# Gated linear attention by half chunks on 64x64 array tiles, ahead of a dropless mixture of experts

## The chip, the cores and the metric

The kernel runs on one core of one Trainium2 chip. The metric is the device time of one execution in microseconds (us). The median of three runs of the kernel before is 489.33 us (488.29 to 489.96).

## The reference

Two blocks stand one behind the other, all in fp32. The first is a recurrence over 768 positions for 4 batches and 8 heads of 48 numbers; its output, seen as 3072 rows of 384, goes through a router with 8 experts, of which each row takes the best one.

```python
B, H, S, D = 4, 8, 768, 48
for t in range(S):
    state = alpha[:, :, t, :, None] * state + np.einsum('bhd,bhe->bhde', k[:, :, t], v[:, :, t])
    y[:, :, t] = np.einsum('bhd,bhde->bhe', q[:, :, t], state)
x = y.transpose(0, 2, 1, 3).reshape(3072, 384)
logits = x @ w_gate                       # 384 x 8
expert_idx = argmax(logits, axis=1)       # gate_w: softmax probability of that expert
out = gate_w[:, None] * (np.maximum(x @ w1[e], 0) @ w2[e])   # e = expert_idx of the row; w1 384x1024, w2 1024x384
```

## The kernel before

**Chunks.** The recurrence is worked in chunks of C = 128 positions: 6 chunks for each of 4 batches, NT = 24 steps in all. With `ln` the logarithm of alpha (`logs`, L199, on ScalarE), one matmul with a triangular matrix gives its running sum inside the chunk (`cums`, L210, PSUM tile `cum`), from which ScalarE makes `icp` and `cp`, the exponentials of minus and plus that sum (L213, L214). GpSimd multiplies k by `icp` and q by `cp` into `kqb` (`operands`, L233, L234), where each head has 64 columns, 48 of them used. TensorE transposes both in pairs of heads (`transposes`, L241, tile `tp`), copied out to `kT` by ScalarE (L246) and to `qT` by VectorE (L244). A tile of 128 partitions holds two heads, one at partition 0 and one at partition 64 (DP = 64); NP = 4 such pairs make up the 8 heads.

**The attention of one step.** `scores` (L254) multiplies kT by qT, 128 x 128 for each head, into `sA` and `sB`. VectorE masks the one with the triangle (L258, `dA`), ScalarE copies the other (L260) and GpSimd masks it (L261, `dB`). `attend` adds into one PSUM tile `y` the product of the carried state `U` with qT (L274, not in the first chunk of a batch) and of v with the masked scores (L280), makes k times v for the state into `kvp` (L291), copies `y` to `yT` on VectorE (L295) and builds the next `U`: an addition on VectorE (L301, or L304 in the first chunk) and a multiplication on GpSimd (L302) with the decay `Eb` of the whole chunk. That decay is the last row of `cp` laid along the partitions: it goes to DRAM and comes back by three small transfers on ScalarE's queue (`decay_out` L218, `decay_in` L226).

**Rows and routing.** `rows` (L313, tile `xr`) turns `yT` back to rows of 384 and multiplies it by the gate's weights in one go, with the matrix `back`. `lgn` (L315, VectorE) sums the logits, `keep_rows` copies the row to `xs` (L320 ScalarE, L321 GpSimd) and stores it in DRAM (`x_rows`, L322). Groups of up to four steps are then routed: `choose` (L328 to L343) takes the best expert, `rank_products` (L348, L349) counts the places of the rows by two fp16 matmuls, `slots_of` (L356 to L364) makes slot numbers, and `one_hots` (L371, L372) makes two fp16 one-hot matrices for each step. After the last step their products (`tokens_of_slots`, L379, and L443 for the counts) give for each slot the row that belongs in it; `indices` (L390, L391) makes `g_idx` of it.

**Order.** Each engine runs its instructions in the order of the program, written out by hand in one loop. Step s of the loop issues loads, `logs(s+5)`, `cums(s+4)`, `operands(s+3)`, `transposes(s+2)`, `rows(s-1)`, `scores(s+1)`, `keep_rows(s-1)`, the decay transfers, `choose`, `attend(s)` and up to two `one_hots`. The loads of alpha, k, q and v (L194, L191: 128 x 8 runs of 192 bytes each), the stores of `x_rows` and the experts' weights (L167, L172) go through the one queue of the sync engine (SP).

**Experts.** The second part gathers rows by an indirect DMA on GpSimd (L499), transposes them (L522), copies them to `xT` (L524) and multiplies them with w1 (L528) and w2 (L553) of the expert; each result goes out by an indirect DMA (L559). Its first matmul needs `g_idx`, the last `x_rows` and the weights of expert 0, which the loop fetches whole at step 15.

Of the kernel before, what the change touches and what calls it, by code (L numbers as in the profile page):

```python
# [18 lines left out]
def kernel(  # L19
# [10 lines left out]
):  # L30

# [42 lines left out]

    consts = ctx.enter_context(tc.tile_pool(name="consts", bufs=1))
    ident = consts.tile([C, C], F32)
    cmask = consts.tile([C, C], F32)
    back = consts.tile([C, NP, D2 + E], F32)
    kqb = [consts.tile([C, 2, H, DP], F32, name=f"kqb{i}") for i in range(4)]
    vb = [consts.tile([C, H, DP], F32, name=f"vb{i}") for i in range(6)]  # L80
    Ub = [consts.tile([C, NP, DP], F32, name=f"Ub{i}") for i in range(2)]
    Eb = [consts.tile([C, NP], F32, name=f"Eb{i}") for i in range(5)]

    def first_consts():
        make_upper_triangular(nc, cmask[:], 1.0, diag=True)
        make_identity(nc, ident[:])
        for t in kqb:
            nc.vector.memset(t[:, :, :, D:], 0.0)
        for t in vb:
            nc.vector.memset(t[:, :, D:], 0.0)  # L90
        for t in Ub + Eb:
            nc.vector.memset(t[:], 0.0)

        for a in range(2):
            r = slice(a * DP, a * DP + D)
            nc.vector.tensor_copy(
                back[r, :, a * D : (a + 1) * D], ident[r, None, a * DP : a * DP + D].to_broadcast([D, NP, D]),
            )
            nc.vector.tensor_scalar_mul(back[r, :, D2:], back[r, :, D2:], -1.0)
# [48 lines left out]
    e_d = nc.dram_tensor("decay_rows", (NT, Dm), F32, kind="Internal").ap()  # L148
# [20 lines left out]

    def fetch2(ex):  # L170
        w2 = wpool.tile([C, FB, Dm], F32, name="w2")
        nc.sync.dma_start(w2[:], moe_w2[bass.ds(ex, 1)].rearrange("e (a p) d -> p (e a) d", p=C))  # L172
        return w2


    with tc.tile_pool(name="ld", bufs=6) as ld, \
         tc.tile_pool(name="work", bufs=2) as work, \
         tc.tile_pool(name="ps", bufs=1, space=PSUM) as ps, \
         tc.manual_schedule():
        st = {s: {} for s in range(NT)}  # L180

# [4 lines left out]
        def load(s, names):  # L186
            for n in names:
                src = rows_of({"a": alpha, "k": k, "q": q, "v": v}[n], s)
                if n == "v":
                    st[s][n] = vb[s % len(vb)]  # L190
                    nc.sync.dma_start(st[s][n][:, :, :D], src)  # L191
                else:
                    t = ld.tile([C, H, D], F32, name=n + "_sb", bufs=4 if n == "a" else 6)
                    nc.sync.dma_start(t[:], src)  # L194
                    st[s][n] = t
# [8 lines left out]
        def heads(t):  # L204
            return t[:].rearrange("s (h d) -> s h d", h=H)

        def cums(s):
            d = st[s]
            cum = ps.tile([C, Dm], F32, name="cum")
            nc.tensor.matmul(cum[:], lhsT=cmask[:], rhs=d["ln"][:], start=True, stop=True)  # L210
            d["icp"] = work.tile([C, Dm], F32, name="icp")
            d["cp"] = work.tile([C, Dm], F32, name="cp", bufs=3)
            nc.scalar.activation(d["icp"][:], cum[:], AF.Exp, scale=-1.0)  # L213
            nc.scalar.activation(d["cp"][:], cum[:], AF.Exp)  # L214

        def decay_out(s):
            if s % NB + 1 < NB:
                nc.scalar.dma_start(e_d[s : s + 1, :], st[s]["cp"][C - 1 : C, :])  # L218

        def decay_in(s):  # L220

            d = st[s]
            if s % NB + 1 < NB:
                d["E"] = Eb[s % len(Eb)]
                for a in range(2):
                    nc.scalar.dma_start(  # L226
                        d["E"][a * DP : a * DP + D, :], e_d[s].rearrange("(p a d) -> a d p", a=2, d=D)[a],
                    )

        def operands(s):  # L230
            d = st[s]
            kq = kqb[s % 4]
            nc.gpsimd.tensor_tensor(kq[:, 0, :, :D], d["k"][:], heads(d["icp"]), op=ALU.mult)  # L233
            nc.gpsimd.tensor_tensor(kq[:, 1, :, :D], d["q"][:], heads(d["cp"]), op=ALU.mult)  # L234
# [12 lines left out]

        def scores(s):
            d = st[s]
            sA = ps.tile([C, NP, C], F32, name="sA")  # L250
            sB = ps.tile([C, NP, C], F32, name="sB")
            for p in range(NP):
                for t, r in ((sA, 0), (sB, DP)):
                    nc.tensor.matmul(  # L254
                        t[:, p, :], lhsT=d["kT"][r : r + D, p, :], rhs=d["qT"][r : r + D, p, :], start=True, stop=True,
                    )
            d["dA"] = work.tile([C, NP, C], F32, name="dA")
            nc.vector.tensor_tensor(d["dA"][:], sA[:], cmask[:, None, :].to_broadcast([C, NP, C]), op=ALU.mult)  # L258
            d["dB"] = work.tile([C, NP, C], F32, name="dB")
            nc.scalar.copy(d["dB"][:], sB[:])  # L260
            nc.gpsimd.affine_select(  # L261
                d["dB"][:], d["dB"][:], compare_op=ALU.is_ge, fill=0.0,
                base=0, pattern=[[0, NP], [1, C]], channel_multiplier=-1,
            )

        def attend(s):

            d = st[s]
            c = s % NB
            y = ps.tile([C, NP, C], F32, name="y")  # L270
            if c > 0:
                for p in range(NP):
                    for r in (0, DP):
                        nc.tensor.matmul(  # L274
                            y[r : r + DP, p, :], lhsT=st[s - 1]["U"][r : r + D, p, :], rhs=d["qT"][r : r + D, p, :],
                            start=(p == 0), stop=False, skip_group_check=True,
                        )
            for p in range(NP):
                for i, r in enumerate((0, DP)):
                    nc.tensor.matmul(  # L280
                        y[r : r + DP, p, :], lhsT=d["v"][:, 2 * p + i, :], rhs=d["d" + "AB"[i]][:, p, :],
                        start=(c == 0 and p == 0), stop=True, skip_group_check=True,
                    )
            d["yT"] = work.tile([C, NP, C], F32, name="yT")
            kvp = ps.tile([C, NP * D + 4 * E], F32, name="kvp")
            kv = kvp[:, : NP * D].rearrange("r (p d) -> r p d", p=NP)
            ranked = [rank_products(g, kvp[:, NP * D : NP * D + len(g) * E]) for g in groups_of if g[-1] == s - 2]
            if c + 1 < NB:
                for p in range(NP):
                    for i, r in enumerate((0, DP)):  # L290
                        nc.tensor.matmul(  # L291
                            kv[r : r + DP, p, :], lhsT=kqb[s % 4][:, 0, 2 * p + i, :], rhs=d["v"][:, 2 * p + i, :D],
                            start=(p == 0), stop=True, skip_group_check=True,
                        )
            nc.vector.tensor_copy(d["yT"][:], y[:])  # L295
            if c + 1 < NB:
                d["U"] = Ub[s % len(Ub)]
                E_b = d["E"][:].unsqueeze(2).to_broadcast([C, NP, D])
                if c > 0:
                    acc = work.tile([C, NP, D], F32, name="acc")  # L300
                    nc.vector.tensor_tensor(acc[:], kv[:], st[s - 1]["U"][:, :, :D], op=ALU.add)  # L301
                    nc.gpsimd.tensor_tensor(d["U"][:, :, :D], acc[:], E_b, op=ALU.mult)  # L302
                else:
                    nc.vector.tensor_tensor(d["U"][:, :, :D], kv[:], E_b, op=ALU.mult)  # L304
            for r in ranked:
                slots_of(*r)

        def rows(s):
# [3 lines left out]
            for p in range(NP):  # L312
                nc.tensor.matmul(xr[:, p, :], lhsT=d["yT"][:, p, :], rhs=back[:, p, :], start=True, stop=True)  # L313
# [3 lines left out]
        def keep_rows(s):  # L317
# [4 lines left out]
            nc.sync.dma_start(x_d[s * C : (s + 1) * C, :], xs[:])  # L322
            del st[s]["xr"]

# [27 lines left out]
        def slots_of(g, pos):  # L352
# [10 lines left out]
            rc = work.tile([C, 2, n], F32, name="rc")  # L363
# [28 lines left out]

        def do(f, i, *a):
            if 0 <= i < NT:
                f(i, *a)

        nc.scalar.preload_act_table_set("natural_log_exp_and_others")
        for i in range(2):
            load(i, "akq")
        nc.gpsimd.memset(back[:], 0.0)  # L400
        for a in range(2):
            nc.scalar.dma_start(
                back[a * DP : a * DP + D, :, D2:], moe_w_gate.rearrange("(p a d) e -> a d p e", a=2, d=D)[a],
            )
        for i in range(2, 4):
            load(i, "akq")
        first_consts()
        hots = []
        for s in range(-5, NT + 1):
            do(load, s + 8 if s + 8 >= 4 else -1, "akq")  # L410
            do(load, s + 5, "v")
            do(logs, s + 5)
            do(cums, s + 4)
            do(operands, s + 3)
            do(transposes, s + 2)
            if s == NT:
# [247 lines left out]
```

## Time and profile before

| what | before |
|---|---|
| median of 3 runs | 489.33 us |
| profiled execution | 489.74 us, of which its span (first to last instruction) is 488.0 |
| TensorE matmul (PE) busy | 457.6 us, 94% of the span, 2881 instructions |
| PEld (weight loads), DVE (VectorE), ACT (ScalarE), POOL (GpSimd) busy | 297.4, 142.3, 103.2, 137.8 us |
| first `y<-dA` of step 0, of step 23 | 21.75 us, 156.6 us from the start |
| first gather of rows issued | 166.67 us |
| first product with w1 | 172.74 us |

All positions are microseconds from the start of the span. PE and PEld are the two halves of TensorE: each fp32 matmul stands as two MATMUL and two LDWEIGHTS instructions, while a transpose is one of each. A group such as `128*64 128x48` is a product with 128 rows and 64 columns of weights through which 48 columns are streamed. [...] durations of neighbours overlap: what a group costs is read from the distance between starts. SPq is the queue of the sync engine: it lists how long the issue of each transfer took.

### The profile page before, as it was taken

How to read it: one execution, taken by the hardware profiler on the slowest of the kernel's cores; microseconds unless marked ns; L12 is line 12 of the kernel's file. 1: busy time of each engine (PE TensorE's matmuls, PEld its weight loads, DVE VectorE, ACT ScalarE, POOL GpSimd, SP SyncE). 2: the span in 40 equal slices, each digit the busy share in tenths (PEclk: the TensorE clock that was granted, in tenths of full speed). 3: DMA queues.
4: the chain of work that ended last, by engine and by line, in shares of the span. 5: the costliest groups of instructions: out<-in, count | busy, mean ns of one | idle time of the engine just before them, and what ended most of it. 6: DMA issues, size and time to landing. Idle time of an engine off the chain costs nothing.

```text
span 488.0 us, 7370 instructions
## 1 busy us (share of the span) xinstructions
PE 457.6 (94%) x2881; PEld 297.4 (61%) x2881; DVE 142.3 (29%) x391; ACT 103.2 (21%) x209; POOL 137.8 (28%) x226
## 2 busy tenths in 40 slices
PE   2999999999999389999999999999999999999992
PEld 0788888888898275555555555555555455555451
DVE  2344766665778421212401201101201201301100
ACT  3544544544421001101001111011111001101010
POOL 3556745555642270010124010016020020010020
PEclk9999999999999779999999999999999999999997
DMA  9999999889992151300726400537300040000000
GB/s 161 199 177 203 207 210 203 168 170 272 299 356 107 50 160 39 142 32 8 267 75 211 135 32 0 189 118 249 129 28 16 1 166 22 1 20 16 2 32 25
DMA packets 127213, 59.76 MB, mean 122 GB/s; under 512 B 110304, under 2 KB 121604, under 8 KB 127178
## 3 DMA queue, kind: packets, MB, share of 16 engines
q1 hardware_dynamic: 114818, 48.87, 39.6%
q0 software_dynamic: 3584, 10.34, 6.4%
q10 hardware_dynamic: 8776, 0.08, 1.0%
q8 instruction: 23, 0.38, 0.3%
q14 instruction: 12, 0.10, 0.1%
HBM read 49.70 MB, written 10.35 MB: 123 GB/s over the span
## 4 chain that ended last, share of the span: by engine, by line
issue 54%; PE 27%; POOL 11%; DVE 2%; DMA 2%; SPq 1%; ACT 0%; POOLq 0%; ACTq 0%
POOL out_dram L559 6%; POOL xg L499 5%; PE sA L254 5%; PE y L280 4%; PE tp L241 4%; PE xr L313 4%; PE cum L210 4%; PE y L274 4%; PE kvp L291 2%; SPq L194 1%; DMA a_sb<-in_alpha_dram 1%; DMA x_rows<-xs 1%; DVE yT L295 1%; DVE sc L330 0%; DVE dA L258 0%
## 5 line engine op out<-in xcount | busy, mean ns | idle before, releaser
L528 PE MATMUL hp<-xT,w 128*128 128x448 f32 (+2 forms) x402 | 148.4, 530 | 1.2 <-DVE xT L524 1.2
L553 PE MATMUL zp<-w,h_sb 128*128 128x384 f32 (+1 forms) x512 | 146.8, 488 | 0.0
L528 PEld LDWEIGHTS hp<-xT,w 128*128 128x128 f32 x402 | 77.4, 194 | 69.9 <-issue 65.0
L553 PEld LDWEIGHTS zp<-w,h_sb 128*128 128x128 f32 (+1 forms) x512 | 81.1, 177 | 62.4 <-issue 13.6
L559 POOL DMA_INDIRECT out_dram<-zo,g_idx x28 | 27.7, 988 | 251.7 <-ACT zo L558 251.7
L542 DVE TENSOR_SCALAR h_sb<-hp 128x448 f32<-128x448 f32 x32 | 20.0, 624 | 218.4 <-PE hp L528 218.4
L544 ACT ACTIVATE h_sb<-hp 128x448 f32<-128x448 f32 x32 | 17.4, 543 | 142.0 <-PE hp L528 142.0
L558 ACT ACTIVATE zo<-zp,gw 128x384 f32<-128x384 f32 x28 | 16.3, 581 | 133.6 <-PE zp L553 129.0
L210 PE MATMUL cum<-ln,cmask 128*128 128x384 f32 x48 | 24.7, 601 | 8.7 <-ACT cp L214 4.4
L499 POOL DMA_INDIRECT xg<-x_rows,g_idx x28 | 26.9, 960 | 12.2 <-issue 12.2
L241 PEld LDWEIGHTS tp<-ident,kqb 128*128 128x128 f32 x192 | 23.5, 146 | 7.9 <-issue 4.2
L254 PE MATMUL sA<-qT,kT 48*128 48x128 f32 x192 | 27.7, 285 | 0.0
L254 PE MATMUL sB<-qT,kT 48*128 48x128 f32 x192 | 27.7, 285 | 0.0
L233 POOL TENSOR_TENSOR kqb<-k_sb,icp 128x384 f32<-128x384 f32 x24 | 23.9, 996 | 8.8 <-ACT icp L213 8.6
L241 PE MATMUL tp<-ident,kqb 128*128 128x128 f32 x192 | 26.2, 282 | 0.0
L280 PE MATMUL y<-dA,vb 128*64 128x128 f32 x192 | 26.1, 279 | 0.0
L280 PE MATMUL y<-dB,vb 128*64 128x128 f32 x192 | 26.1, 279 | 0.0
L313 PE MATMUL xr<-back,yT 128*128 128x104 f32 x192 | 25.4, 275 | 0.7 <-DVE yT L295 0.5
L261 POOL TENSOR_SCALAR_AFFINE_SELECT dB<-dB 128x512 f32<-128x512 f32 x24 | 15.2, 634 | 37.3 <-ACT dB L260 23.8
L254 PEld LDWEIGHTS sA<-qT,kT 48*128 48x128 f32 x192 | 23.1, 187 | 2.6 <-issue 0.3
L313 PEld LDWEIGHTS xr<-back,yT 128*128 128x128 f32 x192 | 23.3, 192 | 1.5 <-issue 1.0
L234 POOL TENSOR_TENSOR kqb<-q_sb,cp 128x384 f32<-128x384 f32 x24 | 23.9, 996 | 0.0
(117 smaller groups left out, 403.0 us busy)
## 6 DMA issues: line engine op xcount, KB each, us to landing
w<-in_moe_w_dram SPq DMA_DIRECT2D x16, 1536.0 KB, 6.8
x_rows<-xs SPq DMA_DIRECT2D x24, 196.0 KB, 2.9
a_sb<-in_alpha_dram SPq DMA_DIRECT2D x24, 192.0 KB, 4.1
k_sb<-in_k_dram SPq DMA_DIRECT2D x24, 192.0 KB, 3.8
q_sb<-in_q_dram SPq DMA_DIRECT2D x24, 192.0 KB, 4.0
vb<-in_v_dram SPq DMA_DIRECT2D x24, 192.0 KB, 4.6
Eb<-decay_rows ACTq DMA_DIRECT2D x40, 0.8 KB, 3.0
xg<-x_rows,g_idx POOLq DMA_INDIRECT x28, 3.1
```

The costliest lines, as they stand in the source:

```text
L210: nc.tensor.matmul(cum[:], lhsT=cmask[:], rhs=d["ln"][:], start=True, stop=True)
L233: nc.gpsimd.tensor_tensor(kq[:, 0, :, :D], d["k"][:], heads(d["icp"]), op=ALU.mult)
L234: nc.gpsimd.tensor_tensor(kq[:, 1, :, :D], d["q"][:], heads(d["cp"]), op=ALU.mult)
L241: nc.tensor.transpose(tp[:, p, :], pair(kqb[s % 4][:, i], p), ident[:])
L254: nc.tensor.matmul(t[:, p, :], lhsT=d["kT"][r : r + D, p, :], rhs=d["qT"][r : r + D, p, :], start=True, stop=True,)
L280: nc.tensor.matmul(y[r : r + DP, p, :], lhsT=d["v"][:, 2 * p + i, :], rhs=d["d" + "AB"[i]][:, p, :], start=(c == 0 and p == 0), stop=True, ...
L313: nc.tensor.matmul(xr[:, p, :], lhsT=d["yT"][:, p, :], rhs=back[:, p, :], start=True, stop=True)
L499: nc.gpsimd.indirect_dma_start(out=xg[:, j, :], out_offset=None, in_=x_d[:, :], in_offset=bass.IndirectOffsetOnAxis(ap=i, axis=0),)
L528: nc.tensor.matmul(hp[:, c0:c1], lhsT=w1[:, a, f * C : (f + 1) * C], rhs=xT[:, a, c0:c1], start=(a == 0), stop=(a == DB - 1), skip_group_c ...
L542: nc.vector.tensor_relu(h[:, f, :cols], hp[:, :cols])
L553: nc.tensor.matmul(zp[i * m : (i + 1) * m, :], lhsT=h[:, f, c0 : c0 + m], rhs=w2[:, f, :], start=(f == 0), stop=(f == FB - 1), skip_group_ ...
L559: ins = nc.gpsimd.indirect_dma_start(out=out[:, :], out_offset=bass.IndirectOffsetOnAxis(ap=idx, axis=0), in_=zo[:], in_offset=None, bound ...
```

## The change

- **Half chunks.** A chunk of 128 positions is worked as two halves j of 64. Scores are 64 x 64 within a half; what the second half owes to the first goes through the state, which is now carried per half: `Ub` holds a state for each half, and k times v (`kv_ps`) is made for each half. The products `inter` (state times qT), `scores`, `kv` and v times scores are 16 matmuls each in place of 8, every one with at most 64 rows and 64 columns of weights and 64 (kv: 48) columns streamed. Their order runs over the four 64x64 tiles of the array in turn. `rows` makes 8 matmuls in place of 4 (64 columns of weights, 104 streamed).
- **Evacuation.** One VectorE instruction masks both heads' scores (`dAB`, 128 x 512); the ScalarE copy and the GpSimd mask are gone. `y` is copied by ScalarE (`results`). VectorE has one more addition in each step (`state`).
- **Decay.** The last row of `cp` is laid along the partitions by 8 matmuls with one streamed column each (`decays`) and one small ScalarE copy. The transfers through DRAM and the tensor `decay_rows` are gone.
- **Order.** kv of step s+1 and y of step s stand at the head of a step, `rows(s)`, the rank products and the routing at its end; `inter(s+1)`, which waits for the copy of `y(s)`, comes after transposes and `cums`. The store of a row is issued at the head of the next step, ahead of its loads; loads run four steps ahead with five buffers each.
- **Constant products.** `keep_busy(n)` issues n matmuls of a zero matrix (128 x 256) that nothing reads: 4 + 4 + 3 + 2 + 1 before the first steps and 11 after the last routing product, ahead of the experts.
- **First weights.** Expert 0's weights come in 12 + 8 parts, one in each step from 6 on (two from 18 on), not whole at step 15.
- **Tail.** The last step's order is written out anew.

The core of the diff:

```diff
+    HALVES = [(j, a) for j in range(2) for a in range(2)]
+    def at(j, a):
+        return DP * (a ^ j)
...
+        def decays(s):
+            last_ps = sums_tile()[:, Dm + 4 * E : Dm + 4 * E + NP]
+            for p in range(NP):
+                for a in range(2):
+                    h = (2 * p + a) * D
+                    nc.tensor.matmul(
+                        last_ps[half(a), p : p + 1], lhsT=cpb[s % 3][DP:, h : h + DP], rhs=ident[DP:, C - 1 :],
+                        start=True, stop=True, skip_group_check=True,
+                    )
+                nc.scalar.copy(st[s]["E"][:], last_ps)
...
+        def inter(s):
+            for p in range(NP):
+                for j, a in HALVES:
+                    if j or s % NB:
+                        nc.tensor.matmul(
+                            y_ps[at(j, a) : at(j, a) + DP, j, p, :],
+                            lhsT=Ub[s % 2][head(a), j, p, :], rhs=d["qT"][head(a), p, half(j)],
...
         def scores(s):
+                for j, a in HALVES:
                     nc.tensor.matmul(
-                        t[:, p, :], lhsT=d["kT"][r : r + D, p, :], rhs=d["qT"][r : r + D, p, :], start=True, stop=True,
+                        sc_ps[half(j), a, p, :], lhsT=d["kT"][head(a), p, half(j)], rhs=d["qT"][head(a), p, half(j)],
...
-            nc.scalar.copy(d["dB"][:], sB[:])
-            nc.gpsimd.affine_select(
...
+            nc.vector.tensor_tensor(
+                d["dAB"][:], sc_ps, m64[:, None, None, :].to_broadcast([C, 2, NP, DP]), op=ALU.mult,
+            )
...
+        def state(s):
+                nc.vector.tensor_tensor(U[:, 1, :, :D], kv_ps[:, 0, :, :], U[:, 0, :, :D], op=ALU.add)
...
+                nc.vector.tensor_tensor(acc[:], kv_ps[:, 1, :, :], U[:, 1, :, :D], op=ALU.add)
+        def results(s):
+            nc.scalar.copy(st[s]["yT"][:], y_ps)
...
+        for s in range(-5, NT - 1):
+            do(store_rows, s - 1)
+            loads(s)
+            if s + 1 >= 0:
+                attend(s)
+            do(state, s + 1)
+            if 0 <= s + 1 < NT and (s + 1) % NB + 1 < NB:
+                decay(s + 1)
+            do(decays, s + 2)
+            do(results, s)
+            do(transposes, s + 2)
+            if s >= 0:
+                do(cums, s + 4)
+                do(operands, s + 4)
...
+            do(inter, s + 1)
+            do(scores, s + 2)
...
+            for _ in range(min(len(hots), 2 if len(hots) > 2 else 1)):
+                one_hots(hots.pop(0))
...
+            do(rows, s)
+            do(keep_rows, s)
...
+            do(logs, s + 5)
...
+        keep_busy(11)
```

## The prediction

> **What bounds the kernel now.** I read the page's busy shares first, then its slices, then busy time by window, then TensorE's timeline of one step, the waits, and SP's timeline. The page:
>
> ```profile
> PE 457.6 (94%) x2881; PEld 297.4 (61%) x2881; DVE 142.3 (29%) x391; ACT 103.2 (21%) x209; POOL 137.8 (28%) x226
> ...
> PE   2999999999999389999999999999999999999992
> PEclk9999999999999779999999999999999999999997
> DMA  9999999889992151300726400537300040000000
> ```
>
> PE is full but for the start and a notch in slices 13 and 14 (159 to 183 us), where its clock falls too. In the first nine slices the DMA engines are full as well. By window (us; busy of PE, PEld, DVE, ACT, POOL; PE clock; DMA share; GB/s):
>
> ```profile
> 63.09:69.26 6.17, 6.17 (x84) 5.41 (x82) 3.19 (x7) 2.84 (x6) 3.19 (x5) 1.00 1.02 190
> ...
> 164.00:170.00 6.00, 0.33 (x2) 0.10 (x1) 1.23 (x7) 0.00 (x0) 2.72 (x3) 0.50 0.16 39
> 170.00:177.60 7.60, 6.64 (x18) 4.89 (x19) 1.11 (x2) 0.00 (x0) 5.77 (x7) 0.50 0.56 157
> ```
>
> The first window is one attention step: PE is never idle, no other engine passes 3.2 of 6.17. The experts begin at half the clock. In that step, on TensorE's timeline:
>
> ```profile
> 64.92 0.27 PE L280 MATMUL y<-dA,vb 128*64 128x128 f32 x1
> 64.93 0.27 PE L280 MATMUL y<-dB,vb 128*64 128x128 f32 x1
> 65.03 0.62 PE L291 MATMUL kvp<-vb,kqb 128*64 128x48 f32 x16
> 65.58 0.91 PE L210 MATMUL cum<-ln,cmask 128*128 128x384 f32 x2
> 66.33 1.04 PE L241 MATMUL tp<-ident,kqb 128*128 128x128 f32 x8
> 67.20 1.04 PE L313 MATMUL xr<-back,yT 128*128 128x104 f32 x8
> ```
>
> Two matmuls on different parts of the array start together (64.92, 64.93; the records say 6.7 ns apart) and the next two follow 0.109 later. Distances between first starts give the step: state products 1.02, y from scores 0.92, kv 0.55, cum 0.75, transposes 0.87, rows 0.97, scores 1.09; sum 6.17. At plain pace (8 pairs at 0.109; kv 8 pairs at 0.058; cum 2 x 0.32; transposes and rows 8 x 0.109) it is 5.48; the other 0.69 lies where the tile shape changes. So the attention is bound by TensorE's stream, and weight loads set its short products: kv streams 48 columns but its pairs run at the 0.058 of 64 weight columns.
>
> Second in line is the transfer queue. At 55 us SP issues one step's five transfers with no gap:
>
> ```profile
> 55.04 0.42 SPq L194 DMA_DIRECT2D a_sb<-in_alpha_dram  x1
> 55.50 0.70 SPq L194 DMA_DIRECT2D k_sb<-in_k_dram  x1
> 56.25 1.08 SPq L194 DMA_DIRECT2D q_sb<-in_q_dram  x1
> 57.43 0.81 SPq L191 DMA_DIRECT2D vb<-in_v_dram  x1
> 58.35 0.90 SPq L322 DMA_DIRECT2D x_rows<-xs  x1
> ```
>
> From 55.04 to 78.19 five such rounds take 23.15, so 4.63 a step: the floor of a step by transfers. At the start ACT waits for alpha, 10.6 us in five waits:
>
> ```profile
> ACT ln L199 <- DMA a_sb<-in_alpha_dram: 10.6, 5, 3.3
> ```
>
> [...]
>
> **The change, part by part.**
>
> *TensorE in a step.* inter, scores, kv and y become 32 instructions each, four tiles in turn. If four run together, 8 rounds at kv's 0.058: 0.46 each, 1.86 in all, against 3.09 at plain pace before (2 x 0.87, 0.90, 0.46). The unseen price has bounds: 0.053 a round (64 columns at the 0.109 per 128) and 0.116 (two tiles at a time). I take 0.058, since four matmuls and four loads at the seen 6.7 ns fit into it. decays adds 16 instructions in 8 pairs, 0.46. rows: 16 in 8 pairs of 104 columns, 0.089 by scaling 0.109: 0.71 against 0.87. cum and transposes stay. Sum 1.86 + 0.46 + 0.71 + 0.87 + 0.64 = 4.54; there are again four changes of shape, so 0.69 more: 5.23. Rank products move but keep their number.
>
> *Other engines in a step,* by mean durations. ACT: loses the dB copy (0.588) and three issues (0.24, 0.31, 0.46), gains the yT copy (0.59) and a small one (about 0.2, by the 128x8 copies): 3.4. DVE: loses the yT copy (0.689), gains one addition (0.349): 3.9 with routing. POOL: loses the select (0.634): 2.9. None passes 5.23, but order counts. ACT waits at xs for lgn, as it did before; behind xs stand ln, the small copy, yT and kT, on which inter and scores of the next step wait. In one step of four two one_hots (1.6) stand ahead of lgn; then inter and scores come some 0.5 late. With choose, 2 us on DVE ahead of the next state, I charge 0.2 a step (bounds 0 and 0.5): **5.43**.
>
> *Transfers.* 4.63 plus a part of 128 or 192 KB from step 6 on: 0.4 to 0.65 at the 200 to 300 GB/s of the page. That is 5.0 to 5.3: hidden behind 5.43, barely, until k and q end at step 16. Without that cover each 0.1 costs 1. The store, now at a step's head, waits on SP for xs and holds four loads behind it; they are wanted four steps later, some 21 us, so that costs nothing while the queue isn't behind. On POOL the decay product now goes ahead of the operands of step s+4, which have two steps until their transposes: nothing.
>
> *Start.* y of step 0 stood behind cum of step 4, the 14th load (its ln began at 17.48); now behind cum of step 3, the 11th (about 14.7), so 18.5 for 21.75: -3.2. The first row store stands on SP behind 31 loads (the 31st was issued at 31.1), lands about 35, and xs has two buffers: step 2 waits for it near 34, +1.5. The constant products cost 4 to 9 us of PE, covered by the 8.7 us that it idles before 12.2. Net -1.7.
>
> *Steps.* Before, y went from 21.75 (step 0) to 141.57 (step 20): 119.8, with three cheap batch heads. Now 20 x 5.43 = 108.6: -11.2. Steps 20 to 23 took 15.0. Two without cum are 5.43 - 0.75 = 4.7 each; the next has kv and y 0.92, a wait of 0.9 for y's copy, inter 0.5 and rows 0.9, so 3.2; 12.6 in all: -2.4.
>
> *Tail.* From the last y to the gather, 156.6 to 166.67, DVE's chain decides: yT, one_hots and slots stood ahead of lgn (161.1). Now ACT copies y and lgn comes ahead of slots: -1.0, bounds -2 and +0.5.
>
> *Clock.* 11 products are 22 instructions, 4.7 us at full clock, between the last routing product and the first turn, 6.1 us later. Warm, the first 18 hp products take 18 x 0.213 = 3.8 and not 6.2: -2.4. If they begin cold, they need up to 8.4 and delay the turns by as much as they save: bounds -2.7 and +0.5.
>
> *Experts:* untouched; the last weight part is issued long before its use.
>
> Sum: -1.7 - 11.2 - 2.4 - 1.0 - 2.4 = -18.7. From the profiled 489.74 (0.4 above the median, 1.7 outside the span) that is **471 us**.
>
> **Rivals.**
> - *No stalls:* DVE and ACT keep up and the store doesn't bite: steps of 5.2, 462. For it: idle engines; against it: waits in order. 0.15.
> - *Transfers or the ACT/DVE order become the bound:* steps of 5.8 up to step 20: +7.4, 478, or up to 484. For it: the full DMA share. With four tiles only partly together (0.07 a round) it comes to the same. 0.2.
> - *Four tiles do not run together* (slower): a round costs two pairs, 0.116, so 4 x 8 x 0.058 = 1.86 more in each of 23 steps, +43: 514[...]. It decides from 0.084 a round, 21 ns a start. Against it: pairs 6.7 ns apart. 0.13.
> - *Gain and cost even out* near that point: 0.04.
> - *Constant products do not warm the clock:* +2.4, inside the range.
>
> **How the numbers follow.** The forecast, 466 to 476, has 0.48. Range 458 to 489: below, no stall and steps at the transfer floor; above, the point of balance. Outside lie the slower case and some 0.05 below. A measurement here tells 0.3% (1.5 us) from no change. Faster 0.83, same 0.04, slower 0.13.
>
> **What would show it.** Rounds of four near 0.058, a step's y to the next at 5.4; y of step 0 near 19 and of step 23 near 141; xs waiting for lgn; SP still without gaps to step 15; full clock at the first hp. Rounds above 0.084, or PE waiting on loads in most steps, would prove me wrong.

## The result, and the profile after

The changed kernel is slower: 508.76 us, median of four runs (503.4 to 512.39), beside 488.84 for the kernel before on the same chip; the ratio is 1.0368 (95% interval 1.0282 to 1.0454). One of the four, 512.39, counts as a slow run, and the ratio leaves it out. The profiled execution took 507.91, its span is 506.1, which is 18.1 more than the 488.0 of before. The page, lines that answer to those shown of before:

```profile
PE 462.4 (91%) x5043; PEld 298.5 (59%) x5043; DVE 132.6 (26%) x398; ACT 106.2 (21%) x229; POOL 126.0 (25%) x205
...
PE   5997996988987788999999999999999999999993
PEclk8899998999997679999999999999999999999997
DMA  9998979899879215230255330255330040000000
```

TensorE is no longer full in the attention (many an 8 or 7 and one 6 in slices 2 to 16, where before had 9 from the second slice to the thirteenth), and its clock drops in more places. Its waits from 30 to 140 us (in all, times, longest):

```profile
PE cum L259 <- issue: 5.6, 2, 4.4
PE y L340 <- issue: 5.2, 4, 2.0
PE scp L330 <- issue: 2.7, 3, 1.4
...
PE cum L242 <- ACT Eb L265: 0.2, 1, 0.2
```

"issue" means that the engine waited for nothing that the profile shows. So TensorE waits, and, but for 0.2 us, not for another engine or a load that it names. The positions say where the 18.1 us are (us; y is the first product of v with the scores):

| stretch | before | after | difference | predicted |
|---|---|---|---|---|
| start to y of step 0 | 21.75 | 26.26 | +4.5 | -3.2, +1.5 later |
| y of step 0 to y of step 20 | 119.82 | 129.96 | +10.1 | -11.2 |
| y of step 20 to y of step 23 | 15.04 | 21.29 | +6.2 | -2.4 |
| y of step 23 to first product with w1 | 16.13 | 15.74 | -0.4 | -1.0 |
| first product with w1 to end of span | 315.3 | 312.9 | -2.4 | -2.4 |

Busy time by window (us from the start; busy of PE, PEld, DVE, ACT, POOL; PE clock; DMA share; GB/s), first of the twenty steps in the kernel before:

```profile
21.75:141.57 119.82, 119.74 (x1553) 104.00 (x1551) 74.53 (x180) 56.14 (x121) 68.96 (x138) 1.00 1.00 220
```

Then of the kernel after: the twenty steps, one undisturbed step, the step behind it, and steps 20 to 23.

```profile
26.26:156.22 129.96, 110.58 (x3327) 92.15 (x3322) 64.78 (x183) 58.54 (x139) 60.65 (x120) 0.98 0.86 196
69.63:74.91 5.28, 5.28 (x183) 4.46 (x178) 3.17 (x8) 2.80 (x7) 2.79 (x5) 1.00 0.92 173
74.91:86.28 11.37, 6.96 (x186) 5.64 (x180) 3.97 (x16) 3.04 (x8) 3.41 (x9) 0.85 0.92 253
156.22:177.51 21.29, 17.56 (x415) 15.70 (x409) 9.08 (x37) 3.92 (x9) 2.00 (x7) 0.66 0.49 162
```

An undisturbed step takes 5.28 with TensorE full, a little under the forecast 5.43. The next holds nearly the same products (186 MATMULs for 183) and takes 11.37. TensorE's timeline (start, duration, line, operation, and in brackets the idle time ahead with what ended it) of both:

```profile
69.63 0.66 PE L340 MATMUL y<-dAB,vb 64*64 64x64 f32 x32
70.12 0.58 PE L259 MATMUL cum<-ident,cpb 64*64 64x1 f32 x16
70.64 1.09 PE L278 MATMUL tp<-ident,kqb 128*128 128x128 f32 x8
...
74.91 0.66 PE L340 MATMUL y<-dAB,vb 64*64 64x64 f32 x32
75.41 0.57 PE L259 MATMUL cum<-ident,cpb 64*64 64x1 f32 x15
80.39 0.26 PE L259 MATMUL cum<-ident,cpb 64*64 64x1 f32 x1 [4.41 <-issue]
80.58 1.75 PE L278 MATMUL tp<-ident,kqb 128*128 128x128 f32 x7
```

The 32 MATMULs of y take 0.49 from first start to the next group (0.06 a round of four): four tiles do run together. But in the second step TensorE stands for 4.41 us in the middle of `decays`, ahead of the 16th of 16 alike instructions, whose operands had long been there, and again "issue" is all that the profile says. A line on the DMA queues that I had not read shows what it waited for. Before, then after (packets, MB, share):

```profile
q8 instruction: 23, 0.38, 0.3%
```

```profile
q8 instruction: 40, 0.66, 0.5%
```

23 packets of 0.38 MB are 16 KB each. TensorE's 2881 MATMUL and 2881 LDWEIGHTS are 5762 instructions, 256 for each of 22.5 packets; after, 10,086 in 40 packets. With the semaphore and control instructions of TensorE's queue the two traces have 5898 and 10,259 records, 23.04 and 40.07 times 256. So in these two traces TensorE's program came 256 instructions at a time. Numbering all these records in order, the stops of the kernel after stand at numbers 193 + 256 n, and between y of step 0 and y of step 23 no other gap from start to start is over 1.1 us; each stop ends 1.3 to 1.7 us after the end of an instruction packet:

```text
block starts  packet starts + takes  next block starts  stop there
 35.16         37.67 + 0.95            40.11              2.26
 68.75         70.24 + 1.38            72.90              0.12
 72.90         78.09 + 0.95            80.39              4.60
119.69        121.67 + 0.88           124.10              1.63
```

In each row the packet starts after the boundary before it is passed (1.49 to 5.19 us after): one block was fetched ahead. A step of the kernel before has some 164 instructions in 6.17 us, so a block lasts 8 to 11 us; a step after has 340 in 5.28, and its blocks, less their stops, last 2.7 to 4.9 at full clock. Between y of step 0 and of step 20, 15 stops at block ends of over 0.5 us make 22.4 us (from start to start); before has none.

### The profile page after: what moved, and what is told of

It reads as the page before. It is cut to its first block, busy times and chain, and to the rows that moved or that the text cites. A ratio compares the mean times of both kernels' runs of the same rounds, so it can differ in the third digit from the quotient of the medians.

```text
span 506.1 us, 11711 instructions
## 1 busy us (share of the span) xinstructions
PE 462.4 (91%) x5043; PEld 298.5 (59%) x5043; DVE 132.6 (26%) x398; ACT 106.2 (21%) x229; POOL 126.0 (25%) x205
## 4 chain that ended last, share of the span: by engine, by line
issue 55%; PE 30%; POOL 9%; DMA 2%; SPq 2%; DVE 1%; ACT 0%; POOLq 0%; ACTq 0%; DVEq 0%
POOL out_dram L675 5%; PE tp L278 5%; PE xr L373 4%; PE cum L242 3%; POOL xg L615 3%; PE scp L330 3%; PE scp L313 3%; PE y L303 3%; PE y L340 3%; PE xr L472 2%; PE cum L259 2%; SPq L227 1%; DMA k_sb<-in_k_dram 1%; PE hp L644 1%; DMA vb<-in_v_dram 1%
## 5 line engine op out<-in xcount | busy, mean ns | idle before, releaser
L675 POOL DMA_INDIRECT out_dram<-zo,g_idx x28 | 27.7, 990 | 250.1 <-ACT zo L674 232.6
L281 DVE COPY qT<-tp 128x512 f32<-128x512 f32 x24 | 16.6, 692 | 41.0 <-PE tp L278 41.0
L242 PE MATMUL cum<-ln,cmask 128*128 128x384 f32 x48 | 21.8, 539 | 4.3 <-ACT ln L231 4.1
L318 DVE TENSOR_TENSOR dAB<-scp,m 128x512 f32<-128x512 f32 x24 | 16.6, 692 | 29.2 <-PE scp L313 29.2
L373 PE MATMUL xr<-back,yT 128*64 128x104 f32 x384 | 23.9, 270 | 0.0
L340 PE MATMUL y<-dAB,vb 64*64 64x64 f32 x768 | 19.1, 233 | 5.2 <-issue 5.2
L259 PE MATMUL cum<-ident,cpb 64*64 64x1 f32 x384 | 15.5, 193 | 9.0 <-issue 9.0
L383 ACT COPY xs<-xr 128x384 f32<-128x384 f32 x24 | 11.5, 479 | 55.8 <-DVE lgn L378 30.9
L271 POOL TENSOR_TENSOR kqb<-q_sb,cpb 128x384 f32<-128x384 f32 x23 | 23.1, 1003 | 0.0
L303 PEld LDWEIGHTS y<-qT,Ub 48*64 48x64 f32 x704 | 14.3, 142 | 13.5 <-issue 9.2
L640 DVE COPY xT<-xtp 128x384 f32<-128x384 f32 (+1 forms) x32 | 14.8, 503 | 25.4 <-PE xtp L638 25.4
```

The source lines that it names most:

```text
L242: nc.tensor.matmul(cum, lhsT=cmask[:], rhs=d["ln"][:], start=True, stop=True, skip_group_check=True)
L259: nc.tensor.matmul(last_ps[half(a), p : p + 1], lhsT=cpb[s % 3][DP:, h : h + DP], rhs=ident[DP:, C - 1 :], start=True, stop=True, skip_gro ...
L271: (nc.gpsimd if s else nc.vector).tensor_tensor(kq[:, 1, :, :D], d["q"][:], heads(d["cp"]), op=ALU.mult)
L303: nc.tensor.matmul(y_ps[at(j, a) : at(j, a) + DP, j, p, :], lhsT=Ub[s % 2][head(a), j, p, :], rhs=d["qT"][head(a), p, half(j)], start=(p = ...
L340: nc.tensor.matmul(y_ps[at(j, a) : at(j, a) + DP, j, p, :], lhsT=d["v"][half(j), 2 * p + a, :], rhs=d["dAB"][half(j), a, p, :], start=(p = ...
L373: nc.tensor.matmul(xr[half(j), p, :], lhsT=d["yT"][:, j, p, :], rhs=back[:, j, p, :], start=True, stop=True, skip_group_check=True,)
```

## Experiments

"Supply" below is the theory that TensorE's instructions arrive too slowly. Its first rival is the prediction's own: four tiles that do not run together. That fell with the 0.06 a round above; what was to be tested is whether the supply makes the loss, and what slows it. The edits are given in short.

**1. The supply by itself.** A kernel of zero products alone: a stream of 64x64 products on four tiles, once without and once beside loads like the kernel's, and a stream of 128-column products on two tiles.

```diff
+ two(64); four(1024)                  # quiet
+ for i in range(84): load 128 x 8 runs of 192 bytes
+ four(1024); two(512)                 # beside the loads
```

> This kernel computes nothing of the reference: it runs streams of fp32 products of zeros on TensorE, 64 products of 128 columns on two tiles, 1024 products of 64 columns on the four 64x64 tiles with no transfer running, then 84 loads in runs of 192 bytes beside 1024 more of them, then 512 of 128 columns on two tiles. Theory A (TensorE's instructions come in blocks of 256, one block ahead, and a block takes longer to arrive than four tiles take to use it): the four-tile stream, 7 ns an instruction between the stops, stops once every 256 instructions also without transfers, for at least 0.5 us each, so a block takes 2.5 us or more in place of 1.9; beside the loads the stops grow to 2 to 4 us; the two-tile stream, 27 ns an instruction and 7 us a block, never stops. Theory B (the stops of the changed kernel are waits for other engines' data that the trace does not name): nothing waits here, so no stops, 1.9 us a block throughout.

TensorE's timeline in the quiet stretch, and windows of the quiet stream, the loaded stream and the two-tile stream (columns as above, without ACT):

```profile
22.84 2.09 PE L34 MATMUL t<-still 64*64 64x64 f32 x128 [1.64 <-issue]
26.84 2.09 PE L34 MATMUL t<-still 64*64 64x64 f32 x128 [1.91 <-issue]
30.57 2.09 PE L34 MATMUL t<-still 64*64 64x64 f32 x128 [1.64 <-issue]
```

```profile
20.00:40.00 20.00, 11.54 (x723) 10.85 (x715) 0.00 (x0) 0.00 (x0) 1.00 0.02 5
80.00:100.00 20.00, 11.04 (x591) 10.34 (x581) 0.00 (x0) 0.00 (x0) 0.91 0.87 171
140.00:160.00 20.00, 20.00 (x370) 20.00 (x368) 0.00 (x0) 0.00 (x0) 1.00 0.95 186
```

The stream goes in groups of exactly 128 MATMULs (with their loads 256 instructions), 14.6 ns from start to start on average (1.87 over 128), and then stops, with the DMA engines idle (share 0.02). A block takes 3.5 to 4.0 us here, 3.8 to 4.6 beside the loads. The two-tile stream, whose blocks need some 7.0 us, is full at a DMA share of 0.95. So a stop needs no other engine and no load: VectorE and GpSimd have x0 in these stretches, and the quiet one stops at a DMA share of 0.02.

**2. Long runs.** Alpha, k and q are read as if each step's 192 KB were one piece (leaves out that they belong to the right heads and rows, so that the experts also get other numbers of rows).

```diff
+ if t is not v: return the flat 128 x 384 block s
```

> The changed kernel, with alpha, k and q loaded as the same number of bytes from one stretch of DRAM, in runs of 1536 bytes and not 192 (so the positions and heads are mixed up: the output is that of other inputs); v as before. Theory A1 (a block of instructions comes late because its transfer queues behind the many small runs): the stops of TensorE at its blocks shrink from some 24 us in all to under 8, and y goes from step 0 to step 20 in some 112 us and not 130. Theory A2 (the block's own delay, from request to use, is enough): stops stay above 15 us. Theory B (waits for data): since loads land sooner, any stop that is a wait for a load goes.

535.48 us, most of the excess in added expert blocks; only the attention counts. Stops at block ends between y of step 0 and step 20 fell from 22.4 to 16.1 us (ten for fifteen), the time between the two stayed (131.0), with the clock halved in four stretches of it, where the kernel after has one and the start of a second (mean clock 0.92 from 26 to 150 us, for 0.98 from 26.26 to 156.22 in the kernel after). The DMA share was 0.61 for 0.86. Long runs alone don't mend it. I took this as a sign that the block's own delay does nearly all the harm, which run 5 corrected.

**3. The same stream in fewer instructions.** inter, scores, kv and y as 4 matmuls each with 256 (kv: 192) columns for 16 with 64 (leaves out the other pairs' weights: each product uses the first pair's). The columns streamed are the same; 8 instructions a product group instead of 32.

```diff
- for p in range(NP): for j, a in HALVES: matmul(y_ps[.., j, p, :], lhsT=v[.., 2p + a, :], rhs=dAB[.., a, p, :])
+ for j, a in HALVES: matmul(y_ps[.., j, :, :], lhsT=v[.., a, :], rhs=dAB[.., a, :, :])
```

> The changed kernel with the same tiles, the same reads, writes and waits and the same streamed columns, but each of the four groups of 16 products issued as 4 products of 256 (kv: 192) columns: it uses the first pair's weights for all four pairs, which leaves out the other pairs' products. TensorE's instructions fall from 340 to about 150 a step at the same array time. Theory A: no stop is left in the steps, y of step 0 to step 20 takes 104 to 112 us in place of 130, the clock stays full until the tail, and the time falls by 22 to 30 us, to 479 to 487. Theory B: the waits for data are all still there, so the time falls by under 6 us.

481.03 us, ratio 0.9832 (0.9795 to 0.987): 27.7 less than the kernel after and faster than the one before. Its windows, y of step 0 to step 20 and one step, and its waits from 123 to 140 us:

```profile
26.20:137.61 111.41, 103.90 (x1474) 72.16 (x1466) 65.37 (x182) 57.08 (x139) 60.23 (x120) 0.97 1.00 208
61.34:66.44 5.10, 5.10 (x81) 3.54 (x74) 3.23 (x8) 2.80 (x7) 2.65 (x5) 1.00 0.96 205
```

```profile
ACT xs L379 <- DMA x_rows<-xs: 7.4, 1, 7.4
...
PE cum L242 <- ACT Eb L265: 5.1, 1, 5.1
```

No stop at a block end is left between these two points. The run takes weight loads away too, but a step without stops is only 0.18 shorter than in the kernel after (5.10 for 5.28), an estimated 3.6 in twenty steps; the other 15 of the 18.6 us less between y and y are, by that estimate, supply, net of a new wait. For the transfers now stand first in line (DMA share 1.00): a row store landed late, ScalarE waited 7.4 us at `xs` for the buffer, and TensorE behind it 5.1, after which its clock was half from 131.39 to 138.22 (0.97 in the mean of the window above).

**4. The gate's transfers ahead of the loads.** In the kernel after, ScalarE's queue:

```profile
3.83 4.60 ACTq L482 DMA_DIRECT2D back<-in_moe_w_gate_dram  x4
8.47 0.52 ACT L231 ACTIVATE ln<-a_sb 128x384 f32<-128x384 f32 x1 [6.40 <-DMA back<-in_moe_w_gate_dram]
```

ScalarE issues four small transfers of gate weights ahead of its first logarithm, and is not through until 8.43: cum of step 0 starts at 9.13, in the kernel before at 4.30.

```diff
+ loads(first step); memset(back); 4 gate transfers
  remaining loads; first_consts()
```

> The changed kernel with the gate's four small transfers on ScalarE's queue, and the GpSimd fill that they wait for, put ahead of the first constants and of all loads but the first. Theory S (the late start is ScalarE standing in the issue of these four transfers from 3.8 to 8.4 us, ahead of the first logarithm): the first logarithm begins at 3.6 to 4.5 in place of 8.5, y of step 0 at 21 to 23 in place of 26.3, and the time falls by 3 to 5 us. Rival (the start is bound by the loads or by the constant products): the first y moves by under 1 us and the time stays.

y of step 0 came at 19.84 for 26.26, y of step 20 at 152.69 for 156.22, and the median is 505.89 (ratio 1.0358, 1.032 to 1.0396), inside the scatter of the kernel after. So the late start is these four issues, with the GpSimd fill that they wait for. The 6.4 us became 3.5 at step 20: an earlier start ran into the same supply (19.4 us of stops at block ends up to there) and into half clock in four stretches, where the kernel after has one and the start of a second (mean clock of the whole span 0.961 for 0.964).

**5. Without the later loads.** From the sixth step on the kernel after uses the tiles of earlier steps again.

```diff
+ if s > AHEAD + 1 - (n != "v"): st[s][n] = st[s - AHEAD - 1][n]   # v: its buffer as it is
+     return
```

> The changed kernel in which only the first five (v: six) steps load their inputs and later steps use those tiles again (leaves out the later inputs; the experts may get other numbers of rows, so only the attention is compared). Weight parts and row stores stay. Open after the runs so far: why a block of 256 TensorE instructions took 4.8 us on average in the changed kernel (from passing one boundary to the restart at the next) when it took 3.5 to 3.7 in a stream without transfers. Theory Q (the instruction packet waits behind the loads on the DMA engines, whatever the size of their runs): blocks fall to about 3.6 us, and at that the changed kernel's own order of instructions, replayed from its trace, loses 3 to 4 us in all; stops at block boundaries under 6 us in sum for 25.7, y of step 0 to y of step 20 about 111 us for 129.96. Theory O (a block's own delay is enough, the loads add little, as the run with long runs seemed to say): stops of 15 to 20 us remain, y to y 120 to 126.

```profile
26.44:140.30 113.86, 107.06 (x3327) 89.72 (x3322) 64.59 (x181) 57.60 (x139) 60.29 (x120) 1.00 0.28 94
```

113.86 us for 129.96 at a DMA share of 0.28 for 0.86, with 8.1 us of stops at block ends for 22.4. Theory Q was the nearer. The mean block that ended in a stop took 4.31 us for 5.27. So an estimated third of the stops (8.1 of 22.4) is the supply's own delay, and two thirds came with the loads; run 2, with long runs, still had 16.1.

**6. The same instructions in another order.**

```diff
- kv, y, decays, transposes, cums, inter, scores, rows
+ kv, transposes, y, decays, cums, inter, rows, scores
```

> The changed kernel with the same instructions in another order: the transposes stand between kv and y, decays and cums ahead of inter, rows between inter and scores, so that the densest 256 instructions of a step take 3.2 us of TensorE's own time for 2.5. Theory R (rate: a step has 340 instructions, a block of 256 takes 4.8 us on average under the loads, so a step takes 6.4 whatever its order): y of step 0 to step 20 stays within 3 us of 129.96, stops sum to 20 to 27, time 503 to 511. Theory B (bursts: only dense stretches outrun the supply): stops under 13 us in sum, time 490 to 498.

525.07 us (ratio 1.0683, 1.0653 to 1.0713), neither theory's number. No stop at a block end over 0.4 us is left up to step 20, but a step takes 7.0:

```profile
75.04:82.04 7.00, 5.77 (x172) 4.59 (x171) 3.10 (x12) 3.01 (x8) 2.60 (x4) 1.00 0.97 286
```

With `scores` last, kv of the next step, which writes the same PSUM tile, has to wait for the mask (`PE scp` behind `DVE dAB`, 0.8 us a step), and `rows` stands closer to the copy of y. TensorE went through its blocks slowly enough for the supply, but because of my new waits. The run doesn't tell rate from bursts.

**7. Fewer instructions, same results.** `decays` as 4 matmuls with 128 weight columns for 8 with 64, `rows` as 4 for 8 (ScalarE turns the second half of y round, in three copies for one): 308 instructions a step.

```diff
- for a in range(2): matmul(last_ps[half(a), p], lhsT=cpb[DP:, h : h + DP], rhs=ident[DP:, C - 1 :])
+ matmul(last_ps[:, p], lhsT=cpb[DP:, 2p : 2p + 2, :], rhs=ident[DP:, C - 1 :])
- nc.scalar.copy(yT, y_ps)
+ nc.scalar.copy(yT[:, :, 0, :], y_ps[:, 0])
+ for a in range(2): nc.scalar.copy(yT[half(a), :, 1, :], y_ps[half(1 - a), 1])
```

> The changed kernel with 32 fewer TensorE instructions in a step (308 for 340) and the same results: the decays by 4 matmuls of 128 weight columns for 8 of 64 (cp is kept with 64 columns a head), and rows by 4 matmuls for 8, since ScalarE turns the second half of y the right way round in three copies for one. Rate theory (blocks of 256 instructions, 4.85 us each under these loads): 308/256 x 4.85 = 5.84 us a step, y of step 0 to step 20 116.7 us for 129.96, stops under 15 us in sum for 25.7, and with fewer stops over 2.5 us less of the half clock: 488 to 495 us (ratio 0.998 to 1.012). Rival (the step is bound by its own waits; ScalarE's two more copies, some 0.5 us, delay inter): y to y stays at 125 to 131, 503 to 509.

509.74 us (1.0396, 1.0369 to 1.0423): no gain. Its profiled execution (515.6) lies above its median, so its distances inside a step are used, and its stops only beside those of run 8:

```profile
69.06:74.96 5.90, 5.90 (x167) 5.10 (x162) 3.26 (x8) 3.46 (x9) 2.75 (x5) 1.00 0.98 263
```

Stops at block ends up to step 20 fell to 6.0 us (5.6 in run 8) as the supply theory had it, but a step without any takes 5.90: from first start to the next group, `decays` needs 0.98 for 0.51 and `rows` 1.07 for 0.88. In `decays`, eight MATMULs that each take two of the 64x64 tiles cost more than sixteen that alternate between these two. What the supply gave back, TensorE's own time took, and the half clock stayed (mean clock 0.954 for 0.964).

**8. The lean kernel with the early start and later weight parts.** Gate transfers as in run 4; the parts of the first weights two a step from step 12.

> The lean kernel with the gate's transfers ahead of the other loads (y of step 0 at 19.8 for 26.3) and the parts of the first weights two a step from step 12 on, when the loads of k and q are about to end, rather than from step 6. If the supply of instructions has room in the lean kernel, the 6.4 us of the start arrive at the end and the lower traffic shortens the blocks: 480 to 484 (ratio 0.981 to 0.99), faster than the kernel before and the one after. Rival (the start runs into the transfers, as 6.4 us shrank to 2 to 3 before): 485 to 491.

505.85 us (1.03, 1.0283 to 1.0317): y of step 0 at 20.40, an undisturbed step 5.90. Of the two theories neither number holds; twenty lean steps of 5.90 are 118 of the 130.5 us from y of step 0 to step 20, with 5.6 of stops and half clock in three stretches beside them (mean clock of the whole span 0.958).

**9. Decays through DRAM again.** 308 instructions a step without the cost of run 7.

```diff
- do(decays, s + 2)
+ do(decay_out, s + 3); do(decay_in, s + 2)     # after keep_rows(s), on ScalarE's queue
```

> The changed kernel with the decays through DRAM again, as in the kernel before: 32 TensorE instructions fewer in a step (308 for 340), and TensorE's own time for a step falls by the 0.51 us that decays took (4.8 for 5.3; in the lean kernel it had risen to 5.9, which hid the rate). Rate theory (blocks of 256 instructions at 4.2 to 4.85 us under the loads, the values of the lean and the changed kernel): 308/256 x 4.2 to 4.85 = 5.1 to 5.8 us a step, y of step 0 to step 20 102 to 117 us for 129.96, and 488 to 497 us; stops at block boundaries stay, since the supply still sets the step. Rival (the three small transfers on ScalarE's queue, 1.0 us of issue a step and waits for slots behind the loads, delay the copies of y and kT): y to y 118 to 130, 498 to 508, with TensorE waiting for ScalarE.

505.9 us (1.0327, 1.0306 to 1.0348), y to y 130.8. Waits from 30 to 140 us:

```profile
PE cum L243 <- ACT ln L232: 10.7, 11, 1.4
...
PE y L339 <- issue: 5.9, 6, 1.6
...
ACT ln L232 <- DMA decay_rows<-cpb: 4.5, 5, 1.4
ACT ln L232 <- DMA Eb<-decay_rows: 4.5, 2, 2.8
```

The rival held, at the upper end of its range (130 for y to y): three small transfers on ScalarE's queue delay `ln`, and TensorE waits for it 11 times. Stops at block ends still sum to 14.3, as the supply theory said.

**10 to 12. The constant products, and the prediction's other gains, on the kernel before.**

```diff
+ 11 matmuls of zeros, 128x256, ahead of indices()          # before_warm; no_warm: the kernel after without them
+ if -4 <= s < 1: do(cums, s + 4)  after attend(s), not ahead  # before_plus, with the 11 products
+ leftover one_hots and slots_of of the last step behind choose # before_plus
```

> The kernel before with 11 constant products (128x256, zero) after its last routing product, ahead of the experts. The prediction's clock term: full clock at the first product with w1, 2.4 us off, 486.5 (ratio 0.995). Rival: they start at half clock, end late and hold the turns back, 488.5 to 490 (ratio 0.999 to 1.002).

> As the one with the 11 constant products, and the running sums of steps 0 to 4 stand at the end of a step rather than ahead of y (the prediction's start term, up to 3.2 us), and in the last step the leftover one-hot matrices and slot numbers stand behind lgn and the choice of the expert (its tail term, 1.0). If the terms hold without the changed kernel's rate of instructions: 2.4 + 3.2 + 1.0 off, 482 to 484. Rival: the start is bound by the transfers, and the steps after it wait for what it gained, so 485 to 487.

> The changed kernel without the 11 constant products at the end of the attention. From the first product with w1 to the end the kernel before took 315.3 us and the changed one 312.9. If the products made that difference (the prediction's clock term): 315.3 again, 2.4 us slower than the changed kernel, 510 to 512. Rival (the gathers' order or the clock's own timing made it; in the kernel before the same products brought 0.8): within 1 us of the changed kernel, 507 to 509.

The first two, like runs 5 and 6, ran on a chip where the kernel before took 492.17. The products alone: 491.43, ratio 0.9984 (0.997 to 0.9998), some 0.8 us. With all three edits: 493.88, ratio 1.0043 (1.0021 to 1.0064), a loss. TensorE's timeline with the products:

```profile
163.59 6.68 PE L451 MATMUL xr<-still 128*128 128x256 f32 x22
170.33 0.97 PE L530 MATMUL xtp<-ident,xg 128*128 128x128 f32 x6
172.14 4.15 PE L536 MATMUL hp<-xT,w 128*128 128x256 f32 x18 [0.84 <-DVE xT L532]
176.13 0.82 PE L530 MATMUL xtp<-ident,xg 128*128 128x128 f32 x6
180.07 4.87 PE L536 MATMUL hp<-xT,w 128*128 128x192 f32 x18 [3.12 <-DVE xT L532]
```

From the first 18 products with w1 to the next group it is 4.0 us for 6.4, the 2.4 less that were forecast, but the second block's come at 180.07 for 180.54: its copy `xT` is late, TensorE idles 3.12, and the clock is halved again from 181.2 to 184.6. Why `xT` was late there and not in the kernel after isn't shown. The kernel after without the products takes 512.37 (ratio 1.0443, 1.04 to 1.0486) with 314.8 from the first product with w1 to the end: its clock is half for that block, as before (0.50 from 172.74 to 176.70 in the kernel before), but the first product comes 0.9 sooner behind y of step 23 (14.86 for 15.74). So the products bring 1.0 net there; the rest of the 3.6 between the medians lies in the attention, where executions of this kernel differ (503.4 to 512.39). In before_plus y of step 0 came 1.3 us earlier, y of step 1 0.6 later and y of step 23 0.8 later than with the products alone. Of the versions that leave nothing out, only the kernel before with the 11 products is faster than the kernel before, by 0.16%.

## Why the prediction was wrong

It forecast 471 us and faster with 0.83.

- **The step that failed: "TensorE in a step".** It priced 340 instructions by when the array could take them, and never by whether they can be had. Its sum for the array was right: 129.96 less 22.4 us of stops at block ends is 107.6, against 20 x 5.43 = 108.6. That it fits so closely is in part luck, since its parts missed: in the undisturbed step the four products took 2.2 for 1.86, `decays` 0.51 for 0.46 and `rows` 0.88 for 0.71, and the 0.69 set aside for changes of shape made up for it. The missing term is the supply: 340 instructions are 1.33 blocks, and at the 3.8 to 4.6 us that a block took beside loads in run 1 that is an estimated 5.1 to 6.1 us a step; 6.5 was measured (129.96 over 20). The size of a block was to be had beforehand: q8 in the page of before counts 23 packets, and 5762 instructions over 23 is 256 less a remainder. The time that a block takes to come was not, since in the kernel before, with 8 to 11 us a block, TensorE never stood at one.
- **The slower rival had the right verdict and the wrong cause, so its hit is luck.** It put 514 (measured 508.76) on tiles that don't run together. Rounds took 0.06, far from its 0.084. The place it pointed to, the distance between starts (21 ns where it decides), was near: within a block an instruction pair took 14.6 ns, but over whole blocks it was 27 to 36 ns per pair in run 1 (3.5 to 4.6 us over 128).
- **Clock.** The prediction read half clock (0.50) in its windows from 164.0 to 177.6 and used it only for the end. From 156.22 to 177.51 the mean clock is 0.66; steps 20 to 23 took 21.29 for the forecast 12.6. In run 3, without stops at block ends, they took 13.7. The granted clock changed at 80.12 and 83.53, 155.21 and 162.04, all on one grid of 3.41 (3.41, 71.68 and 6.83 us apart). In the interval of that grid up to 80.12 TensorE was busy for 0.00 us, in the one up to 155.21 for 0.90, and each time the clock behind it was 0.50; behind the stop of 2.26 us that ended at 40.11 it stayed at 1.00 (35.74 to 42.57). Why half clock lasted two intervals behind 155.21 and one behind 80.12 isn't shown.
- **Start.** The term -3.2 was +4.5. The prediction followed the loads on SP and didn't follow ScalarE's queue, where the order of the first lines of the diff put four gate transfers ahead of `ln`. Run 4 showed it: -1.9 to before, once mended. The +1.5 for the first row store didn't come: from 26 to 60 us ScalarE waited at `xs` for VectorE alone.
- **Right:** the time of a round; full clock for the first 18 products with w1 behind the constant ones (1.00 from 193.25 to 197.30, where before had 0.50; -2.4 beside the kernel before; 1.9 beside run 12, of which 0.9 is paid back by the later turn); xs waiting for lgn (30.9 us in 14 waits, `ACT xs L383 <- DVE lgn L378`); the transfers as the next bound (run 3). **Tail:** -0.4 for -1.0, at a mean clock of 0.84 (before: 0.73).

What the change would have given with enough supply is near the forecast: run 3's 481.0, less 4.5 of the start and 5.1 of its one store wait, would be 471, or 475 with the 3.6 us that its wider products save on TensorE themselves. That sum is an estimate, not a run.

## What to carry to other kernels

Count instructions as a resource: before a product is cut into more and smaller ones, divide 256, the block of these traces, by TensorE's MATMULs and LDWEIGHTS per microsecond, and compare the time that a block will last with the 3.5 to 4.6 us that a block took in run 1, or the 5.3 of the blocks that ended in a stop in the kernel after; the instruction queue's packets in the page (23 for 5898 records, 40 for 10,259) confirmed the block here. A stop put down to "issue" in the middle of alike instructions, at a constant spacing in their number (here 256), was the sign. And a saving in instructions counts only if the wider instruction isn't slower than the ones it replaces, as in the lean kernel (`decays` 0.98 us for 0.51).

## What was not expected of the hardware

- TensorE's instructions came in packets of 16 KB for 256 instructions, one block ahead. In the attention of the kernel after a packet took 0.9 to 1.6 us; it started 0.4 to 5.2 us after the block before it began, and at a stop TensorE went on 1.3 to 1.7 us after its end.
- Four-tile products of 64 columns start 14.6 ns apart on average, LDWEIGHTS included, as long as the block lasts (four some 7 ns apart, the next round of four 58 ns behind the first); over whole blocks it was 27 to 36 ns in run 1. The 21 ns at which the prediction's balance lay is between the two.
- 8 MATMULs on 64 rows by 128 columns with one column streamed took 0.98 us; 16 on 64 by 64 took 0.51, their pairs 58 ns apart, as were the pairs of kv with 64 columns of weights and 48 streamed in the kernel before.
